# Attention into a phase mixer on one core: the first batch's head ordered by hand, its bias added by matmul, its first loads on hardware queues

## The chip, the cores and the metric

The kernel runs on one core of a Trainium2 chip. The metric is the device time of one execution in microseconds (us). Every execution also has a record of the TensorE clock that was granted to it, as a share of full speed. Executions are sorted into fast and slow, and only fast ones are compared here. In the profile PE is TensorE, PEld its weight loads, DVE VectorE, ACT ScalarE, POOL GpSimd, and SP the queue engine.

## The reference

Four batches of attention with eight heads are followed by a mixing layer. What matters of it, cut:

```python
B, H, S, D = 4, 8, 768, 64                     # q, k, v: [B, H, S, D] float32
dist = np.where(is_global & ~is_local, n_local, abs(i - j))
bias = -slopes[:, None, None] * dist           # slopes = 2 ** -(h + 1)
a = softmax(q @ k.T / 8 + bias, where keep = (j < 8) | (0 <= i - j < 96))
x = (a @ v)                                    # -> [B, S, 512]
theta = x @ w_theta
y = w_tok_r @ (x * cos(theta)) + w_tok_i @ (x * sin(theta))
u = x + y
out = u + relu(u @ w_ch)
```

The mask is a band, so for each tile of 128 keys the kernel computes only the scores of that tile's own 128 queries and of the next tile's; there are six such tiles, and all but the last have both parts.

## The kernel before

The work is done for pairs of heads ("pair" from here on; four pairs to a batch). Per pair, `prep` copies q and k into the order that PE transposes, and DVE or ACT copies them out of PSUM as qT and kT; kG is a copy of kT with the eight global keys put in. `scores` does the matmuls for a third of the tiles, one exp on ACT, and one multiply on DVE with `etab`, which holds exp(bias). `values` multiplies with v, normalises and writes x. `xtrans` transposes x for `theta`, whose sines and cosines are the last ACT work before the mixing matmuls can run. I call everything up to the sixth sine and cosine of batch 0 the head. Cuts are marked.

```python
    alloc_loads(0)                      # all loads of q, k, v: POOL's software queue, float32 -> bf16
    load_qk(0, 0, 2); load_qk(0, 2, 2); load_v(0, 0, 4)
    load_qk(0, 4, 2); load_qk(0, 6, 2); load_v(0, 4, 4)
    # ... ident and dist from a scan, a transpose and comparisons, on DVE

    def bias_table(p):
        for h in (2 * p, 2 * p + 1):
            nc.scalar.activation(etab[:, h, 0:3], dist, AF.Exp, scale=-slopes[h])
        # ... two of the five blocks are copied on DVE

    def scores(b, p, c):
        # ... matmuls of qT with kT and kG into pb (PSUM), start=True, stop=True
        ins = nc.scalar.activation(e_c, pb[:, :, 0:n], AF.Exp, scale=scale).ins
        # ... behind the last exp of a batch: a small Sin, which loads the sine table early
        nc.vector.tensor_mul(e_c, e_c, tab[...])          # one of two forms

    # the head: order set by hand on PE alone, the other engines left to the scheduler
    with tc.manual_schedule(engines={mybir.EngineType.PE}):
        warm(8)                                            # matmuls on zeros
        prep(0, 0, 4)
        distances()
        bias_table(0)
        for p in range(1, NP + 1):
            if p < NP:
                prep(0, p, 2 if p == 1 else 0)
                bias_table(p)
            if p == 2:
                vglob(0, 0, 4)                             # vG: copy of v with the global keys
            if p == 3:
                vglob(0, 4, 4)
            for c in range(NT // 2):
                scores(0, p - 1, c)
                if p == 1:
                    warm(1)
            if p > 1:
                values(0, p - 2, 0)
                values(0, p - 2, 1)
            if p > 2:
                xtrans(0, p - 3, nc.scalar.copy)
        # ... the last values, xtrans, and the first transposed token weights
    # ... then theta(0), and mixing of batch b woven with the attention of batch b + 1
```

The softmax here doesn't subtract the row's maximum and nothing guards it: scores larger than these inputs give would overflow.

Of the kernel before, what the change touches and what calls it, by code (L numbers as in the profile page):

```python
# [9 lines left out]
FP = mybir.dt.float32  # L10
BF = mybir.dt.bfloat16
# [5 lines left out]
def kernel(  # L17
# [61 lines left out]
                            in_=v[b, h0:h0 + n].rearrange("h (t p) d -> p (h t) d", p=T))  # L79


    alloc_loads(0)
    load_qk(0, 0, 2)
    load_qk(0, 2, 2)
    load_v(0, 0, 4)
    load_qk(0, 4, 2)
    load_qk(0, 6, 2)
    load_v(0, 4, 4)
    zero = const.tile([T, 512], BF)
    nc.vector.memset(zero, 0.0)  # L90

    ones = const.tile([T, 2 * T], FP)
    nc.vector.memset(ones, 1.0)
    ramp = const.tile([T, 2 * T], FP)
    nc.vector.tensor_tensor_scan(ramp, ones, ones, -1.0, op0=ALU.mult, op1=ALU.add)
    kmod = const.tile([T, GS], FP)
    nc.vector.transpose(kmod, ramp[:, 0:GS])
    pidx = const.tile([T, 1], FP)
    for p in range(NP):
        nc.vector.tensor_scalar(pidx[GS * p:GS * (p + 1), :], kmod[GS * p:GS * (p + 1), 0:1],  # L100
                                float(GS * p), None, op0=ALU.add)
    ident = const.tile([T, T], BF)
    nc.vector.tensor_scalar(ident, ramp[:, 0:T], pidx, None, op0=ALU.is_equal)






    assert NG <= T - NL and NG <= GS  # L110
    dist = const.tile([T, 3, T], FP)
    far = const.tile([T, 2 * T], FP)
    near = const.tile([T, 2 * T], FP)

    def distances():
        nc.vector.tensor_scalar(near, ramp, pidx, None, op0=ALU.subtract)
        nc.vector.tensor_scalar(far, near, 0.0, None, op0=ALU.is_lt)
        nc.vector.scalar_tensor_tensor(far, in0=near, scalar=float(NL), in1=far,
                                       op0=ALU.is_ge, op1=ALU.add)
        nc.vector.scalar_tensor_tensor(dist[:, 2], in0=far[:, 0:T], scalar=1e6, in1=near[:, 0:T],  # L120
                                       op0=ALU.mult, op1=ALU.max)
        nc.vector.scalar_tensor_tensor(dist[:, 1], in0=far[:, T:2 * T], scalar=1e6,
                                       in1=near[:, T:2 * T], op0=ALU.mult, op1=ALU.max)
        nc.vector.tensor_copy(out=dist[:, 0], in_=dist[:, 2])
        nc.vector.tensor_scalar(dist[0:NG, 0], dist[0:NG, 2], float(NL), None, op0=ALU.min)
        nc.vector.memset(dist[0:NG, 1], float(NL))


    etab = const.tile([T, H, 5, T], BF)

    def bias_table(p):
        for h in (2 * p, 2 * p + 1):
            nc.scalar.activation(etab[:, h, 0:3], dist, AF.Exp, scale=-slopes[h])
        hs = slice(2 * p, 2 * p + 2)
        nc.vector.tensor_copy(out=etab[:, hs, 3:5], in_=etab[:, hs, 1:3])

    halfpi = const.tile([T, 1], FP)
    junk = const.tile([T, 1], FP)
# [34 lines left out]

    anchor = {}

    def behind(eng):

        return tc.issue_after(anchor[eng]) if eng in anchor else nullcontext()

    def prep(b, p, w=0):  # L180
        qk = loads[b][0]
        if (b, 0) not in qkT:
            x_sb[b] = moe.tile([T, NP, NT, T], BF, name="x_sb", bufs=2)
            xT_sb[b] = moe.tile([T, NC, S], BF, name="xT", bufs=1)

        qkn = att.tile([T, NT, 2, 2, D], BF, name="qkn", bufs=3)
        with behind("dve"):
            for i_ in range(2):
                (nc.scalar.copy if b == 0 and i_ and p < 2 else nc.vector.tensor_copy)(  # L189
                    out=qkn[:, :, i_].rearrange("p t h d -> p h t d"), in_=qk[:, i_, 2 * p:2 * p + 2])  # L190
        qT = att.tile([T, S], BF, name="qT", bufs=6)
        kT = att.tile([T, S], BF, name="kT", bufs=6)
        kG = att.tile([T, NT - 2, T], BF, name="kG", bufs=6)
        for i_, dst in ((0, qT), (1, kT)):
            ps = ps_small([T, NT, T], BF)
            with behind("pe"):
                for t_ in range(NT):
                    nc.tensor.transpose(ps[:, t_, :], qkn[:, t_, i_].rearrange("p h d -> p (h d)"), ident)  # L198

            dst = dst.rearrange("p (n t) -> p n t", t=NT)  # L200
            src = ps.rearrange("p t n -> p n t")
            if i_ == 0:
                nc.vector.tensor_copy(out=dst, in_=src)  # L203
            else:
                nc.scalar.copy(out=dst, in_=src)  # L205
            if w:
                warm(w)

        nc.vector.tensor_copy(out=kG, in_=kT[:, T:(NT - 1) * T].rearrange("p (t n) -> p t n", t=NT - 2))
        nc.vector.tensor_copy(out=kG[:, :, 0:NG], in_=kT[:, None, 0:NG].to_broadcast([T, NT - 2, NG]))  # L210
        qkT[(b, p)] = (qT, kT, kG)

    ebuf = {}

    def scores(b, p, c):
        qT, kT, kG = qkT[(b, p)]
        if c == 0:
            ebuf[(b, p)] = att.tile([T, 2, NT, 2, T], BF, name="e", bufs=4)
        e_t = ebuf[(b, p)]
        pb = ps_big()  # L220
        for j in range(2):
            jt = 2 * c + j
            own = slice(jt * T, (jt + 1) * T)
            nxt = slice((jt + 1) * T, (jt + 2) * T)
            for part in range(2 if jt + 1 < NT else 1):
                for hh in range(2):
                    R = slice(D * hh, D * (hh + 1))
                    lhsT = kG[R, jt - 1, :] if part and jt else kT[R, own]
                    o = (2 * j + part) * T
                    nc.tensor.matmul(pb[:, hh, o:o + T], lhsT=lhsT, rhs=qT[R, (own, nxt)[part]],  # L230
                                     start=True, stop=True)
        n = min(4, 2 * NT - 1 - 4 * c) * T
        e_c = e_t[:, :, 2 * c:2 * c + 2].rearrange("p a j s n -> p a (j s n)")[:, :, 0:n]
        ins = nc.scalar.activation(e_c, pb[:, :, 0:n], AF.Exp, scale=scale).ins  # L234
        if c == NT // 2 - 1 and p == NP - 1:

            with tc.issue_after(ins):
                nc.scalar.activation(junk, halfpi, AF.Sin)
        tab = etab[:, 2 * p:2 * p + 2]
        if c == 0 or n < 4 * T:  # L240
            s0 = 0 if c == 0 else 2
            nc.vector.tensor_mul(e_c, e_c, tab[:, :, s0:s0 + n // T].rearrange("p a s n -> p a (s n)"))  # L242
        else:
            e4 = e_t[:, :, 2 * c:2 * c + 2].rearrange("p a j s n -> p a j (s n)")
            nc.vector.tensor_mul(
                e4, e4, tab[:, :, 2:4].rearrange("p a s n -> p a (s n)")[:, :, None, :].to_broadcast(
                    [T, 2, 2, 2 * T]))

    vGs, pos = {}, {}

# [52 lines left out]

    def theta(b, c, j):
        if c == 0 and j == 0:
            zri[b] = moe.tile([T, 2, NT, DM], BF, name="zri", bufs=1)
        xT, xb = xT_sb[b], x_sb[b]
        if j == 0:
            pss["th"] = ps_big()
# [5 lines left out]
        if j == 1:  # L315
            cs = moe.tile([T, 2, 2, DM], BF, name="cs")
            nc.scalar.activation(cs[:, 0], pb, AF.Sin, bias=halfpi)  # L317
            nc.scalar.activation(cs[:, 1], pb, AF.Sin)
            for i_ in range(2):
                for j_ in range(2):  # L320
                    nc.vector.tensor_mul(  # L321
                        zri[b][:, i_, 2 * c + j_, :].rearrange("p (g d) -> p g d", g=NP),
                        xb[:, :, 2 * c + j_, :],
                        cs[:, i_, j_].rearrange("p (g d) -> p g d", g=NP))
# [81 lines left out]

    load_w()
    load_all(1)
    with tc.manual_schedule(engines={mybir.EngineType.PE}):
        warm(8)  # L410
        prep(0, 0, 4)
        distances()
        bias_table(0)
        for p in range(1, NP + 1):
            if p < NP:
                prep(0, p, 2 if p == 1 else 0)
                bias_table(p)
            if p == 2:
                vglob(0, 0, 4)
            if p == 3:  # L420
                vglob(0, 4, 4)
            for c in range(NT // 2):
                scores(0, p - 1, c)
                if p == 1:
                    warm(1)
            if p > 1:
                values(0, p - 2, 0)
                values(0, p - 2, 1)
            if p > 2:
                xtrans(0, p - 3, nc.scalar.copy)  # L430
        values(0, NP - 1, 0)
        values(0, NP - 1, 1)
        xtrans(0, NP - 2, nc.scalar.copy)
        xtrans(0, NP - 1, nc.scalar.copy)
        trans_w(0, nc.scalar.copy)
    rest = []
    for b in range(B):
        nxt = b + 1 if b + 1 < B else None
# [3 lines left out]
        th = [lambda c=c, j=j: theta(b, c, j) for c in range(NT // 2) for j in range(2)]  # L442
        pre = [lambda p=p: prep(nxt, p) for p in range(NP)] if nxt else []
        if b == 0:
            order = th
        elif nxt:
            order = rest[:-1] + pre[:2] + th[:2] + pre[2:] + th[2:3] + rest[-1:] + th[3:]
        else:
# [20 lines left out]
            rest.insert(1, lambda b=b: utrans(b, NT - 1))  # L469
    for f in rest:  # L470
        f()


# [33 lines left out]
```

## Time and profile before

| kernel before | us |
|---|---|
| time, median of the first 3 runs | 190.88 (190.42 to 191.08) |
| span of the profiled run | 189.6 |
| first exp of batch 0 starts | 14.41 |
| last exp of batch 0 ends | 29.33 |
| first of the six sines and cosines starts | 35.49 |
| the sixth ends | 41.56 |
| first exp of batch 1 starts | 54.22 |

These are the milestones. The first lines of the page of the kernel before give busy time by engine; the rows of digits give the busy share of 40 equal slices in tenths, and PEclk is the granted clock, also in tenths:

```profile
PE 167.9 (89%) x1500; PEld 89.1 (47%) x1523; DVE 137.9 (73%) x309; ACT 102.9 (54%) x122; POOL 27.1 (14%) x31
...
PE   7855787899999999999939999999999999999981
...
PEclk9999669999999999999987999999999999999999
```

From the ninth slice (38 us) on, PE is full except for one stretch near 95 us, so the span after the head is PE's. In the head PE has digits of 5 to 8. An earlier end of the head therefore moves the whole rest forward. The same head in windows, for the kernel before (columns: the window, its length, busy us of PE, PEld, DVE, ACT, POOL with counts, then the clock, the DMA share and GB/s):

```profile
10.00:20.00 10.00, 5.88 (x95) 4.01 (x95) 7.62 (x21) 8.25 (x13) 5.89 (x8) 1.00 1.63 189
20.00:30.00 10.00, 8.20 (x131) 6.73 (x128) 8.83 (x24) 8.85 (x12) 3.99 (x3) 0.66 1.16 209
```

Over these windows no engine is full, DVE and ACT both run near 9 of 10 us in the second one, and the clock falls to 0.66 there. Windows of half the length show more: from 15 to 25 us DVE is busy all the time (5.00 of 5 us twice) and ACT nearly so (5.00 and 4.80). The chain of waits of the kernel before in the head (start, duration, what; each piece released the next):

```profile
4.20 8.16 DMA vn<-in_v_dram
...
12.38 0.43 DVE vG L259
12.81 0.20 DVE kG L209
...
14.41 2.64 ACT e L234 x3
...
18.15 0.94 ACT e L234
...
19.13 0.34 PE pb L230 x6
19.47 0.92 PE ps L278 x22
20.39 1.29 PE ps L198 x12
...
21.71 0.80 ACT kT L205
22.51 0.94 ACT e L234
```

The first exp waits, through kG, for v: the scheduler put the vG copy ahead of the kG copy on DVE, and v lands at 12.36. And from 18 us on the chain goes round a loop of ACT and PE once a pair: exp, scores (L230), values (L278), the twelve transposes of the next pair (L198), the kT copy, exp. One turn is 22.51 - 18.15 = 4.4 us. PE's weight loads and matmuls are not the limit in themselves: PE had idle time in both windows.

### The profile page before, as it was taken

The page shows a single profiled execution, that of the slowest core. Times are in us where ns is not written, and L with a number is a line of the kernel's source. Part 1 is how long each engine was busy: PE and PEld are TensorE (multiplying, and loading weights), DVE is VectorE, ACT ScalarE, POOL GpSimd, SP SyncE. Part 2 cuts the span into 40 slices and gives each one's busy share as a digit, 9 for nine tenths or more (in the row PEclk, how much of TensorE's full clock was granted, in tenths as well). Part 3 has the DMA queues.
Part 4 walks back from the last instruction along what each step waited for, and adds up shares of the span by engine and source line. Part 5 has one row for each costly group of instructions (what it writes and reads, how often), then busy time and mean ns, then how long its engine had stood idle before and what let it go on. Part 6 is the DMA issues. An engine that isn't in the chain of part 4 may idle for free.

```text
span 189.6 us, 3693 instructions
## 1 busy us (share of the span) xinstructions
PE 167.9 (89%) x1500; PEld 89.1 (47%) x1523; DVE 137.9 (73%) x309; ACT 102.9 (54%) x122; POOL 27.1 (14%) x31
## 2 busy tenths in 40 slices
PE   7855787899999999999939999999999999999981
PEld 2424665445656555654414454644454544434430
DVE  5839987386999997998853786998877864734422
ACT  2469988871397684598724360499663604800010
POOL 7974361300040004020000000000000000000000
PEclk9999669999999999999987999999999999999999
DMA  4999999999999983999991337301165374113432
GB/s 63 153 188 181 210 209 207 204 189 142 130 83 182 225 116 75 148 142 146 223 116 58 74 91 185 109 3 55 28 66 141 88 145 148 59 32 107 118 106 111
DMA packets 58081, 23.97 MB, mean 126 GB/s; under 512 B 44240, under 2 KB 54992, under 8 KB 58064
## 3 DMA queue, kind: packets, MB, share of 16 engines
q0 software_dynamic: 35760, 12.85, 70.6%
q1 hardware_dynamic: 22304, 10.88, 25.0%
q8 instruction: 12, 0.20, 0.5%
q14 instruction: 5, 0.04, 0.1%
HBM read 25.69 MB, written 6.29 MB: 169 GB/s over the span
## 4 chain that ended last, share of the span: by engine, by line
PE 55%; ACT 14%; DVE 13%; DMA 12%; issue 2%; POOL 2%; ACTq 0%; POOLq 0%
PE ps L332 22%; PE ps L357 10%; DMA uT<-u 8%; PE pb L313 7%; ACT e L234 6%; PE pb L230 5%; DMA vn<-in_v_dram 4%; PE pb L278 4%; DVE qT L203 4%; ACT cs L317 3%; PE ps L198 3%; DVE qkn L189 2%; PE ps L278 2%; DVE zri L321 2%; POOL qk L72 2%
## 5 line engine op out<-in xcount | busy, mean ns | idle before, releaser
L234 ACT ACTIVATE e<-pb 128x1024 bf16<-128x1024 f32 (+1 forms) x48 | 44.1, 958 | 25.8 <-PE pb L230 25.7
L332 PE MATMUL ps<-zri,w_tokT_111 128*128 128x512 bf16 x141 | 53.6, 381 | 0.9 <-issue 0.3
L332 PE MATMUL ps<-zri,w_tokT_110 128*128 128x512 bf16 x130 | 49.5, 382 | 1.3 <-DVE zri L321 0.8
L337 DVE TENSOR_TENSOR u<-x_sb,ps 128x512 bf16<-128x512 bf16 x24 | 16.5, 687 | 16.6 <-PE ps L332 16.0
L357 PE MATMUL ps<-w_ch_bf,uT 128*128 128x512 bf16 x94 | 25.3, 391 | 3.7 <-DMA uT<-u 3.5
L360 DVE SCALAR_TENSOR_TENSOR o_sb<-ps,u 128x512 f32<-128x512 f32 x24 | 16.5, 687 | 11.4 <-PE ps L357 11.4
L313 PE MATMUL pb<-w_theta_bf,xT 128*128 128x512 bf16 x93 | 23.6, 379 | 0.7 <-ACT xT L299 0.4
L321 DVE TENSOR_TENSOR zri<-x_sb,cs 128x512 bf16<-128x512 bf16 x48 | 18.3, 421 | 7.2 <-ACT cs L317 6.1
L242 DVE TENSOR_TENSOR e<-e,etab 128x1024 bf16<-128x1024 bf16 (+1 forms) x32 | 19.7, 617 | 3.5 <-ACT e L234 3.5
L230 PE MATMUL pb<-qT,kT 64*128 64x128 bf16 x224 | 17.9, 231 | 4.7 <-ACT e L234 4.6
L332 PEld LDWEIGHTS <-w_tokT_110 128*128 128x128 bf16 x144 | 14.1, 98 | 15.2 <-issue 1.1
L332 PEld LDWEIGHTS <-w_tokT_111 128*128 128x128 bf16 x144 | 14.1, 98 | 13.2 <-issue 0.5
L205 ACT COPY kT<-ps 128x768 bf16<-128x768 bf16 x16 | 12.9, 805 | 13.4 <-PE ps L198 13.4
L230 PEld LDWEIGHTS <-kT 64*128 64x128 bf16 x224 | 10.0, 99 | 18.3 <-issue 16.7
L351 ACT COPY uT<-ps 128x512 bf16<-128x512 bf16 x7 | 4.1, 587 | 26.1 <-PE ps L350 26.1
L317 ACT ACTIVATE cs<-pb,halfpi 128x1024 bf16<-128x1024 f32 x12 | 13.4, 1120 | 8.9 <-issue 6.8
L278 PEld LDWEIGHTS <-e 128*128 128x128 bf16 x352 | 14.7, 100 | 6.8 <-issue 1.0
L198 PE MATMUL ps<-ident,qkn 128*128 128x128 bf16 x192 | 16.1, 232 | 1.1 <-DVE qkn L189 0.9
L198 PEld LDWEIGHTS <-qkn 128*128 128x128 bf16 x192 | 12.8, 103 | 8.4 <-DVE qkn L189 6.1
L230 PE MATMUL pb<-qT,kG 64*128 64x128 bf16 x128 | 13.6, 228 | 2.0 <-DVE kG L210 2.0
L203 DVE COPY qT<-ps 128x768 bf16<-128x768 bf16 x16 | 15.2, 947 | 0.0
L357 PEld LDWEIGHTS <-uT 128*128 128x128 bf16 x96 | 8.4, 99 | 13.5 <-DMA uT<-u 4.7
(63 smaller groups left out, 204.3 us busy)
## 6 DMA issues: line engine op xcount, KB each, us to landing
out_dram<-o_sb SPq DMA_DIRECT2D x24, 256.0 KB, 2.3
qk<-in_q_dram POOLq DMA_DIRECT2D x3, 768.0 KB, 8.1
qk<-in_k_dram POOLq DMA_DIRECT2D x3, 768.0 KB, 13.6
vn<-in_v_dram POOLq DMA_DIRECT2D x3, 768.0 KB, 22.7
w_nat<-in_moe_w_tok_r_dram POOLq DMA_DIRECT2D x3, 384.0 KB, 13.6
w_nat<-in_moe_w_tok_i_dram POOLq DMA_DIRECT2D x3, 384.0 KB, 14.8
qk<-in_q_dram POOLq DMA_DIRECT2D x4, 192.0 KB, 6.4
qk<-in_k_dram POOLq DMA_DIRECT2D x4, 192.0 KB, 6.7
```

Of the source, the lines that this page charges most:

```text
L198: nc.tensor.transpose(ps[:, t_, :], qkn[:, t_, i_].rearrange("p h d -> p (h d)"), ident)
L203: nc.vector.tensor_copy(out=dst, in_=src)
L230: nc.tensor.matmul(pb[:, hh, o:o + T], lhsT=lhsT, rhs=qT[R, (own, nxt)[part]], start=True, stop=True)
L234: ins = nc.scalar.activation(e_c, pb[:, :, 0:n], AF.Exp, scale=scale).ins
L242: nc.vector.tensor_mul(e_c, e_c, tab[:, :, s0:s0 + n // T].rearrange("p a s n -> p a (s n)"))
L278: nc.tensor.matmul(o, lhsT=l_, rhs=r_, start=(i_ == 0), stop=(i_ == len(mms) - 1))
L313: nc.tensor.matmul(pb[:, j, :], lhsT=xT[:, dc, st * T:(st + 1) * T], rhs=w_theta_bf[:, dc, :], start=(dc == 0), stop=(dc == NC - 1))
L317: nc.scalar.activation(cs[:, 0], pb, AF.Sin, bias=halfpi)
L321: nc.vector.tensor_mul(zri[b][:, i_, 2 * c + j_, :].rearrange("p (g d) -> p g d", g=NP), xb[:, :, 2 * c + j_, :], cs[:, i_, j_].rearrange( ...
L332: anchor["pe"] = nc.tensor.matmul(ps, lhsT=w_tokT[wi][:, st, tt * T:(tt + 1) * T], rhs=zri[b][:, wi, st, :], start=(st == 0 and wi == 0), ...
L337: anchor["dve"] = nc.vector.tensor_add(u_sb[b, tt].rearrange("p (g d) -> p g d", g=NP), x_sb[b][:, :, tt, :], ps.rearrange("p (g d) -> p g ...
L357: nc.tensor.matmul(ps_c, lhsT=uT[:, dc, :], rhs=w_ch_bf[:, dc, :], start=(dc == 0), stop=(dc == NC - 1))
```

## The change

The intent is a shorter head: order every engine by hand there, get the first q and k sooner, take work off DVE and ACT. In five parts:

1. **Loads.** q and k of pair 0 come as float32 through hardware queues (issued by SP and ACT), and are cast on chip. The other loads stay on POOL's software queue.
2. **Bias on PE.** In batch 0 the bias is put into PSUM by a matmul (a diagonal of -slope/scale times `dist`), and the score matmuls add to it. The twelve multiplies with `etab` go. So do 17 of the 23 warm-up matmuls.
3. **Tables out of the head.** `etab` is needed from batch 1 on only, so its eight exps come behind the sixth sine, 640 columns wide for 384 before.
4. **Order.** Casts of pair p+2 and its transposes are issued one pair earlier, kG never stands behind vG.
5. **Set-up.** An iota on POOL replaces a scan on DVE for `ident` and `dist`.

The core of the diff, with cuts:

```diff
-    load_qk(0, 0, 2)
+    qk32 = moe.tile([T, 2, 2, NT, D], FP, name="qk32", tag="zri", bufs=1)
+    for i_, eng in ((1, nc.sync), (0, nc.scalar)):
+        eng.dma_start(out=qk32[:, i_]..., in_=(q, k)[i_][0, 0:2]...)
+    nc.gpsimd.iota(near, pattern=[[1, 2 * T]], base=0, channel_multiplier=-1, ...)
 ...
+    def score_bias(p, c):
+        pb = pbs[0, p, c] = ps_big()
+        for hh in range(2):
+            nc.tensor.matmul(pb[:, hh, 0:n * T], lhsT=diag[:, 2 * p + hh],
+                             rhs=dist[:, s0:s0 + n]..., start=True, stop=False)
 ...
-                                     start=True, stop=True)
+                                     start=bool(b), stop=bool(b) or (...))
 ...
+        if b == 0:
+            return                       # no multiply with etab in batch 0
 ...
-    with tc.manual_schedule(engines={mybir.EngineType.PE}):
-        warm(8)
-        prep(0, 0, 4)
-        ...
+    warm(6)                              # all five engines by hand
+    distances(); diagonals(0)
+    # pair 0: casts, transposes and copies split in halves over DVE and ACT
+    kglob(0, 0)
+    score_bias(0, 0); score_bias(0, 1)
+    score_mms(0, 0, 0); score_mms(0, 0, 1)
+    score_exp(0, 0, 0)
+    # casts, diagonals and transposes of pair 1
+    for p in range(NP):
+        nxt = p + 1 < NP
+        score_exp(0, p, 1)
+        if nxt:
+            out0(p + 1, 1, act)          # kT on ACT
+            out0(p + 1, 0, dve)          # qT on DVE
+            kglob(0, p + 1)
+        if p:
+            values(0, p - 1, 0); values(0, p - 1, 1)
+        score_bias(p, 2); score_mms(0, p, 2); score_exp(0, p, 2)
+        if p + 2 < NP:
+            # casts on DVE, diagonals(p + 2)
+        # vglob(0, 0, 4) at p == 0, vglob(0, 4, 4) at p == 1
+        if nxt:
+            # scores 0 and 1 of pair p + 1, exp 0
+            if p + 2 < NP:
+                turn0(p + 2, 1); turn0(p + 2, 0)
+        if p:
+            xtrans(0, p - 1, act if p == NP - 1 else dve)
+    # ... values, trans_w, xtrans, theta(0)
+    for p in range(NP):
+        bias_table(p)
```

## The prediction

> **What bounds the kernel now.** The span is 189.6 us. From 37 us on it is TensorE's: the windows show PE busy 95 to 99% from 40 to 80 us and from 100 to 160 us. Before that nobody is full (10 to 20 us: PE 5.9, DVE 7.6, ACT 8.3). The chain of waits in this head runs POOL issues (to 4.2 us), the v load (lands 12.4), DVE copies, first exp at 14.4, then exps in groups of three at 14.4, 18.0, 22.4, 26.7 (a period of 4.1 us), last exp ending 29.3, six sines from 35.5 to 41.6, full mixing from about 42.5. The first exp is late because kG stands behind vG, which waits for v. The DMA share is 99% nearly everywhere from 5 to 55 us; batch 1's q and k land at 39.0 and 42.9 and are first cast at 46.9.
>
> **What the change does.**
> - DVE loses 12 etab multiplies in batch 0 (0.54 to 0.68 us, 7.6 us) and the scan chain (about 1.6 us); it gains 8 small diagonals and xT copies.
> - ACT loses two 0.83 us casts, and the tables (3.9 us) move behind the sines, wider (640 for 384 columns: estimate 8 x 0.65 us plus one 1.28 us table load).
> - PE gains 24 bias matmuls of 512 or 384 columns (0.216 us step warm, 0.43 as in the first warm-ups: 4.8 to 9 us) and loses 17 warm-ups.
> - k0 and q0 come through hardware queues: estimate landed by 4 to 4.6 us, against 4.7 and 6.7.
> - kG no longer stands behind v.
>
> Replaying the new order by hand with these durations: with a quick iota the first exp starts at about 7.5 us, the sines end at 35 to 39 us, against 41.6: 3 to 6 us gained, all critical, as the later PE-bound phase merely starts earlier.
>
> **The catch.** The changed program has a library reload on POOL ahead of the iota; the old has none. The Trainium skill, "GPSIMD Engine Reference", section Instruction dispatch, gives about 6 us for the first call to a freshly loaded kernel; this trace cannot check it. If it holds, ident, dist and every software-queue load come some 6 to 7 us later: the first exp at 13 to 14 us, v at 17 to 18, the last exp at 30 to 32, the sines end at 41 to 45, batch 1's k lands near 48. The gain is then gone, up to 3 us worse. I hold that more likely than not (0.6).
>
> **Second risk.** Warm-ups vanish. The granted clock falls to 0.66 from 20 to 30 us even so; the skill's "TensorE: Matmul & The Clock Gate", Part 1, says idleness halves the clock. Cold, the bias matmuls put PE on the head's critical path.
>
> **Time.** Quick iota: about 186. Slow: about 191.5. Together 189.5, range 184.5 to 196. Faster by over 2%: 0.31; within 2%: 0.45; slower: 0.24.
>
> **What would show it.** POOL's timeline: does the first software load issue before 3 us or after 8? The first exp's start; the end of the sixth sine; PE idle before batch 1's transposes (late loads); the granted clock from 10 to 35 us; uT copies behind the eight table exps.
>
> **What would make it wrong.** A hidden reload; a clock that stays low; a changed collision of uT transposes with loads (the chain holds 8.6 us of it at 90 us).

## The result, and the profile after

The changed kernel took 186.06 us (median of 4 runs, 185.80 to 186.38), the kernel before 190.98 beside it (190.42 to 192.26). The ratio is 0.9731, with a 95% interval of 0.9688 to 0.9775: faster. Here and below a ratio is the mean time of one kernel's fast runs over that of the other's fast runs of the same rounds, so it is not quite the ratio of the medians that I quote.

| milestone in the profiled run, us | before | after | gain |
|---|---|---|---|
| first exp starts | 14.41 | 9.31 | 5.10 |
| last exp of batch 0 ends | 29.33 | 25.14 | 4.19 |
| first sine starts | 35.49 | 29.93 | 5.56 |
| sixth ends | 41.56 | 36.01 | 5.55 |
| first exp of batch 1 | 54.22 | 48.77 | 5.45 |
| span | 189.6 | 184.0 | 5.6 |

The gain is complete at the sixth sine and is carried to the end unchanged. It does not come from a faster pace of the pairs: from the first exp to the end of the last the four pairs took 14.92 us before and 15.83 after. The changed kernel starts 5.1 us earlier, gives 0.9 of it back, and wins 1.4 between the last exp and the first sine. The same lines of the page, for the kernel after:

```profile
PE 166.5 (90%) x1505; PEld 86.9 (47%) x1530; DVE 134.4 (73%) x299; ACT 102.3 (56%) x120; POOL 25.6 (14%) x30
...
PE   5889879999999999998769999999999999999981
...
PEclk9999999999999999999978999999999999999998
```

Busy totals hardly moved, so this is not less work but less waiting: PE's digits reach 8 in the second slice and 9 from the seventh. The windows of the kernel after, same columns:

```profile
10.00:20.00 10.00, 8.85 (x139) 5.66 (x138) 8.51 (x26) 8.77 (x11) 4.43 (x7) 1.00 1.56 193
20.00:30.00 10.00, 8.39 (x117) 5.07 (x119) 6.63 (x18) 6.60 (x9) 4.05 (x3) 1.00 1.16 209
```

PE does 8.85 us in place of 5.88 between 10 and 20 us, and DVE and ACT have become free for a third of the next window, with the multiplies and tables gone and the last exp over by 25.14 us. The clock stays at 1.00. The chain of waits in the head of the kernel after:

```profile
0.74 4.19 DMA qk<-in_k_dram
4.95 0.52 ACT qkn L187
...
5.52 1.46 PE ps L193 x12
6.98 1.71 PE pb L246 x4
...
9.31 1.94 ACT e L273 x2
11.25 0.70 ACT kT L200
...
14.75 0.70 ACT kT L200
...
16.11 0.56 DVE x_sb L333
```

The wait for v is gone; the first exp now hangs on k's load, its cast, the transposes and four bias matmuls (L246). The first two kT copies on this chain lie 3.5 us apart, in place of the old loop's 4.4, but that is not the average: see the 15.83 us above. From 15.5 to 22.5 us the chain then stays on DVE, without a gap. The later stages have the old shape: the one stall of PE, at a DMA transpose of u, lasts 8.63 us after and 8.61 before.

### The profile page after: what moved, and what is told of

Same layout as the page of the kernel before. It is cut to its first block, busy times and chain, and to the rows that moved or that the text cites. A ratio compares the mean times of both kernels' runs of the same rounds, so it can differ in the third digit from the quotient of the medians.

```text
span 184.0 us, 3698 instructions
## 1 busy us (share of the span) xinstructions
PE 166.5 (90%) x1505; PEld 86.9 (47%) x1530; DVE 134.4 (73%) x299; ACT 102.3 (56%) x120; POOL 25.6 (14%) x30
## 4 chain that ended last, share of the span: by engine, by line
PE 55%; DVE 14%; ACT 14%; DMA 9%; issue 6%; ACTq 0%
PE ps L377 23%; PE ps L402 10%; DMA uT<-u 6%; ACT e L273 5%; PE pb L358 5%; PE pb L266 5%; PE pb L323 4%; ACT cs L362 4%; PE ps L225 4%; DVE x_sb L333 3%; DMA qk<-in_k_dram 2%; ACT cs L363 2%; DVE zri L366 2%; PE ps L157 1%; DVE qT L230 1%
## 5 line engine op out<-in xcount | busy, mean ns | idle before, releaser
L377 PE MATMUL ps<-zri,w_tokT 128*128 128x512 bf16 x271 | 70.0, 383 | 1.6 <-issue 0.6
L377 PEld LDWEIGHTS <-w_tokT 128*128 128x128 bf16 x288 | 25.5, 98 | 28.3 <-issue 1.7
L266 PEld LDWEIGHTS <-kT 64*128 64x128 bf16 x224 | 9.1, 95 | 17.4 <-issue 14.9
L396 ACT COPY uT<-ps 128x512 bf16<-128x512 bf16 x7 | 4.1, 586 | 22.5 <-PE ps L395 22.4
L283 DVE TENSOR_TENSOR e<-e,etab 128x1024 bf16<-128x1024 bf16 (+1 forms) x24 | 14.8, 617 | 1.9 <-ACT e L273 1.7
L232 ACT COPY kT<-ps 128x768 bf16<-128x768 bf16 x12 | 9.7, 808 | 10.5 <-PE ps L225 10.3
L78 POOL DMA_DIRECT2D vn<-in_v_dram x5 | 9.6, 1915 | 29.7 <-DVE rec L331 17.1
L358 PEld LDWEIGHTS <-xT 128*128 128x128 bf16 x96 | 8.8, 98 | 10.1 <-issue 1.3
L323 PE MATMUL pb<-vn,e 128*128 128x65 bf16 x168 | 12.2, 195 | 0.6 <-ACT e L273 0.4
L363 ACT ACTIVATE cs<-pb 128x1024 bf16<-128x1024 f32 x12 | 12.3, 1026 | 0.0
L333 DVE TENSOR_TENSOR x_sb<-pb,rec 128x768 bf16<-128x768 f32 x12 | 11.5, 955 | 0.3
## 6 DMA issues: line engine op xcount, KB each, us to landing
w_nat<-in_moe_w_tok_i_dram POOLq DMA_DIRECT2D x3, 384.0 KB, 15.5
```

The costliest lines, as they stand in the source:

```text
L266: nc.tensor.matmul(pb[:, hh, o:o + T], lhsT=lhsT, rhs=qT[R, (own, nxt)[part]], start=bool(b), stop=bool(b) or (jt == NT - 1 or (j == 1 and ...
L323: nc.tensor.matmul(o, lhsT=l_, rhs=r_, start=(i_ == 0), stop=(i_ == len(mms) - 1))
L333: nc.vector.tensor_mul(xv, po4[:, :, :, 0:D], rec.to_broadcast([T, n, NT, D]))
L358: nc.tensor.matmul(pb[:, j, :], lhsT=xT[:, dc, st * T:(st + 1) * T], rhs=w_theta_bf[:, dc, :], start=(dc == 0), stop=(dc == NC - 1))
L363: ins = nc.scalar.activation(cs[:, 1], pb, AF.Sin).ins
L377: anchor["pe"] = nc.tensor.matmul(ps, lhsT=w_tokT[wi][:, st, tt * T:(tt + 1) * T], rhs=zri[b][:, wi, st, :], start=(st == 0 and wi == 0), ...
```

## The experiments

Twelve kernels ran, all with correct results. The milestones are of the profiled run. "Mean" is of the timed fast runs. Means are compared only with the ratio's own partners: the kernel before took 190.47 as a mean beside e1 to e4, 192.05 beside e5 to e8, 190.46 beside e9 to e11, 191.26 beside e12.

| run | what | first exp | last exp ends | sixth sine ends | span | mean | ratio to before (95%) |
|---|---|---|---|---|---|---|---|
| before | | 14.41 | 29.33 | 41.56 | 189.6 | | 1 |
| after | | 9.31 | 25.14 | 36.01 | 184.0 | 186.08 | 0.9731 (0.9688 to 0.9775) |
| e1_swload | after, software loads | 10.93 | 27.45 | 38.33 | 186.4 | 187.93 | 0.9866 (0.9797 to 0.9935) |
| e2_dvebias | after, multiplies and tables back | 9.36 | 29.76 | 42.24 | 189.3 | 192.34 | 1.0097 (0.9968 to 1.0226) |
| e3_bfence | before, kG ahead of vG | 12.27 | 29.53 | 43.01 | 191.2 | 193.20 | 1.0142 (1.0081 to 1.0204) |
| e4_warm10 | after, ten warm-ups | 9.32 | 25.41 | 36.30 | 184.7 | 185.38 | 0.9713 (0.9628 to 0.9799) |
| e5_bwarm | before, more fillers | 14.57 | 29.42 | 41.67 | 188.5 | 190.57 | 0.9923 (0.9874 to 0.9972) |
| e6_bfencewarm | e3 and e5 together | 11.63 | 29.20 | 41.45 | 187.8 | 189.18 | 0.9851 (0.9798 to 0.9903) |
| e7_biota | before, an unused iota | 16.80 | 29.55 | 41.84 | 189.9 | 193.00 | 1.0050 (0.9979 to 1.0121) |
| e8_tabhead | after, tables back | 9.37 | 26.33 | 39.29 | 185.7 | 188.38 | 0.9809 (0.9757 to 0.9861) |
| e9_kgact | after, first kG on ACT | 8.36 | 24.52 | 35.4 | 183.3 | 185.16 | 0.9732 (0.9652 to 0.9812) |
| e10_kgact10 | e9 and e4 together | 8.41 | 24.35 | 35.2 | 184.0 | 184.73 | 0.9709 (0.9623 to 0.9795) |
| e11_combo | e10 and more off DVE | 8.43 | 24.17 | 34.9 | 183.5 | 185.54 | 0.9751 (0.9678 to 0.9825) |
| e12_bpebias | before, bias on PE | 14.70 | 29.68 | 41.14 | 188.2 | 189.68 | 0.9906 (0.9867 to 0.9945) |

The theories at the start were these. The **start** theory: the old head was late because kG stood behind v; an earlier first exp is the gain. The **loads** theory: it is the hardware-queue loads. The **DVE** theory: it is the removed multiplies and tables. The **clock** theory: it is the half clock between 20 and 30 us. And the open branch of the prediction: what the iota costs POOL.

### e7_biota: the old kernel with an iota that nothing uses

```diff
+    idle = const.tile([T, 2 * T], FP)
+    nc.gpsimd.iota(idle, pattern=[[1, 2 * T]], base=0, channel_multiplier=-1,
+                   allow_small_or_imprecise_dtypes=True)
     alloc_loads(0)
```

> The old kernel with one unused iota, and so one library reload, on POOL ahead of all loads. My prediction's slow branch says that the first software load is issued 6 us or more later and the total is 195 us or more. The changed kernel's trace (iota 0.33 us, 0.4 us of wait ahead of it) says 0.3 to 0.6 us later and a total within 0.7 us of the old kernel.

POOL's timeline has it (start, duration, engine, line, operation), first of the kernel before, then of e7, then of the kernel after:

```profile
1.25 0.81 POOL L72 DMA_DIRECT2D qk<-in_q_dram  x1 [0.81 <-POOLq L488]
```

```profile
0.84 0.34 POOL L83 IOTA idle<- 128x256 f32 x1 [0.39 <-POOLq L491]
1.35 0.84 POOL L72 DMA_DIRECT2D qk<-in_q_dram  x1 [0.18 <-issue]
```

```profile
0.84 0.33 POOL L92 IOTA near<- 128x256 f32 x1 [0.39 <-POOLq L578]
1.36 0.84 POOL L72 DMA_DIRECT2D qk<-in_q_dram  x1 [0.19 <-issue]
```

The iota starts at 0.84 us and the first software load is issued at 1.35, only 0.10 us later than without it. The time, 1.0050 with an interval that holds 1, shows no cost of several us. The first exp came later here, at 16.80, but the last exp did not (29.55), which is a first hint of a result below. It is no more than a hint, because the scheduler also reordered the rest: all eight table exps ran from 6.10 us on, ahead of the first exp, where the kernel before had spread them over the pairs. So the branch that I had held more likely fell: in these runs the iota and its reload together put the first load off by about 0.1 us. What can be seen of a reload: the traces of both runs hold two MODIFY_POOL_CONFIG instructions of POOL's queue, of 11 ns each, at 0.74 and 0.78 us (the timeline leaves them out, a query by the iota's line lists them), and the kernel before has none. The iota starts 0.05 us after the second. Whether code was loaded ahead of the span, or was there already, these records do not show.

### e1_swload: the changed kernel with pair 0 on the software queue again

```diff
-    qk32 = moe.tile(...)
-    for i_, eng in ((1, nc.sync), (0, nc.scalar)):
-        eng.dma_start(out=qk32[:, i_]..., ...)
     alloc_loads(0)
+    load_qk(0, 0, 2, (1, 0))
     load_qk(0, 2, 2)
-        src = qk32[:, i_] if p == 0 else loads[0][0][:, i_, 2 * p:2 * p + 2]
+        src = loads[0][0][:, i_, 2 * p:2 * p + 2]
```

> The changed kernel, only its first pair back on the software queue (bf16, k first, then q; everything else as changed). If the hardware loads carry the gain, the first exp starts about 2.5 us or more later than the changed kernel's 9.3 us and the total is 188.5 us or more. If the order and the bias carry it, k and q land within about 1.5 us of the hardware loads (the old kernel's first two took 3.5 and 4.6 us from issue), the first exp is about 1 us later and the total is 186.5 to 187.5 us.

The casts of e1 on ACT show when k and q were there:

```profile
4.95 0.51 ACT L184 COPY qkn<-qk 128x384 bf16<-128x384 bf16 x1 [2.93 <-DMA qk<-in_k_dram]
7.25 0.51 ACT L184 COPY qkn<-qk 128x384 bf16<-128x384 bf16 x1 [1.79 <-DMA qk<-in_q_dram]
```

k came no later than in the changed kernel (cast at 4.95 in both). q came at 7.25; in the changed kernel the cast of q starts by 5.4. The two loads land 2.3 us apart on the software queue and nearly together on the two hardware queues. The first exp is 1.6 us later, the last exp, the sines and the span 2.3 to 2.4 us. That lies between what the order and the loads theories expected: about 2.4 of the 5.6 us hang on the loads, and the rest does not. Pair 0 is not the whole of it. With pair 0 back on the software queue all later loads are issued behind it, and the chain of waits of e1 runs through k of pair 2 (issued at 6.45, in the changed kernel at 5.06):

```profile
6.45 8.77 DMA qk<-in_k_dram
```

DVE sat idle for 1.15 us before the cast of it at 15.24, where the changed kernel had this cast at 12.39 without a wait. So moving two loads to other queues also brought the loads of the other pairs forward.

### e2_dvebias: the changed kernel with multiplies on DVE and tables on ACT in the head

```diff
-    score_bias(0, 0)
-    score_bias(0, 1)
+    bias_table(0)
 ...
+        score_mul(0, p, 0)
+        score_mul(0, p, 1)          # the multiplies with etab, three per pair
 ...
-    for p in range(NP):
-        bias_table(p)               # behind the sines
```

> The changed kernel, with batch 0's bias back as a multiply on DVE and the tables back on ACT in the head; loads and hand order kept, no bias matmuls. If the bias on PE matters for the pace of the four pairs, DVE (7.6 us more) and ACT (5 us more) lengthen the head by 3 to 5 us: 189 to 191 us, and with fewer matmuls the granted clock dips below 1.0 between 10 and 30 us as it did before. If only the early start matters, the first exp stays near 9 us and the total within 1 us of 186.

The first exp is as early as in the changed kernel, 9.36, and the last exp ends at 29.76, later than in the kernel before. The sixth sine ends 6.2 us later than in the changed kernel. So in this form an early start is worth nothing at the end of the head. The chain of waits of e2, one pair's turn and the transposes before and after it:

```profile
14.29 1.48 PE ps L193 x12
...
15.78 0.96 DVE qT L200
...
17.15 0.59 DVE e L287
17.74 0.60 DVE e L290
...
20.06 1.46 PE ps L193 x12
```

DVE carries qT, kG (cut), two multiplies and x (cut) in one line, and the transposes take 1.46 to 1.48 us, as they do at half clock. The windows of e2 give a clock of 0.85 from 20 to 30 us and 0.81 from 30 to 40, where the changed kernel has 1.00. Even that is too kind: the trace's first record of a full clock in e2 is at 23.55 us (8.93 in the changed kernel), the views print the unrecorded time before it as 1.00, and the transposes at 14.29 and 20.06 say that PE was still at half clock. e8 below, which has the bias matmuls, keeps 1.00 in both. That suggests that they also keep PE warm, with 17 warm-ups fewer. It also means that e2 does not measure multiplies and tables alone: three groups of transposes on its chain took 1.41 to 1.48 us where one at full clock took 0.84 (e9), so by an estimate from these figures about 1.8 us of its delay are the clock's. The timed mean has only two fast runs (191.03 and 193.65) and carries less weight than the milestones.

### e8_tabhead: only the tables back in the head

```diff
         score_exp(0, p, 2)
+        bias_table(p)
 ...
-    for p in range(NP):
-        bias_table(p)
```

> The changed kernel with only the exp tables moved back into the head, two (0.65 us each) behind the last exp group of each pair on ACT; bias stays on PE. If ACT has no room there, the pairs' period rises from 4.05 to 4.7 us, the last exp ends 2 to 2.5 us later and the total is 187.5 to 188.5 us, although 6.4 us of tables behind the sines are gone. If ACT's gaps take them in, the total is within 0.5 us of 186.

The last exp moved by 1.2 us, less than expected; the total of 188.41 as median was as expected, but partly for another reason. The chain of waits of e8 behind the last exp:

```profile
26.34 1.28 ACT L277
...
27.85 1.28 ACT L131
...
31.91 1.28 ACT L362
```

These are three loads of ACT's function table. My edit put the last pair's tables behind the small sine that loads the sine table early, so exp and sine tables were loaded once more each. Of the 3.3 us by which the sixth sine came later, about 2.6 (2 x 1.28) are my edit's own fault, so e8 overstates what tables cost at that milestone. And its span lost only 1.7 us: it had no clock dip near 100 us (see e5 below), and no tables behind the sines. What stands is the last exp: the tables cost the head 1.2 us there. In e2 tables, multiplies and the half clock together cost 4.6; an estimate for the multiplies and the clock against bias on PE, inside the new order, is the difference, 3.4 us, if they add. With the 1.8 us put down to the clock above, some 1.6 would be left for the multiplies; no run separates the two.

### e3_bfence: the old kernel with vG held behind the first kG

```diff
+        kg_ins[b, p] = nc.vector.tensor_copy(
+            out=kG[:, :, 0:NG], in_=kT[:, None, 0:NG].to_broadcast([T, NT - 2, NG])).ins
 ...
-        with behind("dve"):
+        with tc.issue_after(kg_ins[0, 0]) if b == 0 and h0 == 0 else behind("dve"):
```

> The old kernel, with one fence: vG of the first four heads comes behind kG of the first pair on DVE, so that the first scores no longer wait for v. If the DVE order is what made the first exp late, it starts near 12.3 us in place of 14.4, and if the pace then holds, the total falls by about 2 us to 189. If the pairs are paced by DVE, ACT or the clock, the start moves and the last exp does not: under 0.5 us gained.

The first exp came 2.1 us earlier, the last exp 0.2 us later, and the kernel was slower (1.0142). The windows of e3, as above:

```profile
20.00:30.00 10.00, 8.31 (x121) 7.19 (x119) 9.78 (x25) 7.14 (x9) 4.75 (x4) 0.50 1.16 209
```

The start theory falls as far as an early first exp alone goes: DVE is full (9.78) from 20 us on although the exps began earlier, and PE is at half clock for the whole window. That left a doubt that the clock had eaten the gain, which e5 and e6 were made for. A third cause shows in the trace, and I had not asked for it: between 11 and 17 us DVE sat idle for 2.9 us in front of casts of pairs 2 and 3 that waited for their q and k (2.18, 0.50 and 0.19 us), while the first multiply, whose exp had long ended, stood behind these casts in its queue and began at 16.91.

### e5_bwarm and e6_bfencewarm: the old kernel with fillers, without and with the fence

```diff
                 scores(0, p - 1, c)
-                if p == 1:
-                    warm(1)
+                if p < 4:
+                    warm(1 if p == 1 else 2)
```

e6 is this edit and e3's.

> The old kernel with filler matmuls behind the scores of pairs 1 and 2 too (two per group, as it already has one per group for pair 0). If the half clock from 20 to 27 us is on the path of the old head, the granted clock stays near 1.0 there, the last exp ends 1 us or more before 29.3 us and the total falls by about 1 us. If the pairs are paced by DVE and ACT alone, the clock rises and nothing else changes (under 0.4 us).

> The old kernel with the vG fence of the earlier run and the fillers as well. The fence alone started the first exp 2.1 us earlier and lost it all, with the granted clock at 0.50 from 20 to 30 us. If the clock ate it, this run ends its last exp at 27 to 28 us and the total is about 2 us below the old kernel. If DVE and ACT ate it, the last exp stays at 29 us or later and the total is not below the old kernel's.

The fillers did raise the clock to 1.00 from 20 to 30 us in both runs. The last exp ended at 29.42 and 29.20, against 29.33: nothing was gained in the head. So taking away the late start, the low clock or both was not enough in the old kernel. The chain of waits of e6 says what came next (cut):

```profile
7.72 8.48 DMA qk<-in_k_dram
...
16.22 0.36 DVE qkn L190
16.58 0.60 DVE e L244
```

In e6 it is first the load of pair 3's k, which lands at 16.19 and whose cast stands ahead of the first multiply on DVE (DVE idled 2.98 us in front of pair 2's casts as well), and then DVE with the twelve multiplies, 9.67 us busy of 10 from 20 to 30. In the old kernel's runs with the multiplies the first of them began at 16.05 (before), 16.53 (e5), 16.49 (e6), 16.91 (e3) and 17.86 us (e7), whenever the first exp came, and the last exp ended within 0.4 us in all five. The chain of the kernel before runs through the ACT and PE loop of 4.4 us instead, but DVE is full there too. So several limits lie close together: the load of pair 3 with the casts ahead of the multiplies, DVE's work behind it, and the loop. An early start with the multiplies ahead of those casts was not run, so it stays open what it would gain.

Yet both runs were faster by the clock on the wall, e5 by 0.8%, e6 by 1.5%, with heads that had not moved. Comparing later milestones settles where, for the profiled runs. From the start of batch 1's last cosine pair (third activation with the half-pi bias) to the start of batch 2's first lie 36.58 us in the kernel before, 35.44 in e5 and 34.98 in e6. The windows there, first of the kernel before, then of e5:

```profile
90.00:100.00 10.00, 6.60 (x66) 3.10 (x66) 6.45 (x12) 4.58 (x6) 0.00 (x0) 0.92 1.08 163
100.00:110.00 10.00, 9.90 (x99) 4.87 (x100) 6.07 (x10) 4.45 (x5) 0.00 (x0) 0.91 0.31 85
```

```profile
90.00:100.00 10.00, 6.25 (x67) 3.01 (x67) 6.53 (x12) 4.67 (x6) 0.00 (x0) 1.00 1.15 166
100.00:110.00 10.00, 9.89 (x112) 5.38 (x114) 6.69 (x11) 4.91 (x5) 0.00 (x0) 1.00 0.36 95
```

PE stalls on the DMA transpose of u in both (6.60 and 6.25 us busy of 10), and behind the stall it runs at half clock for a while in one and not in the other. Over the profiles of before, after and all twelve experiments, the four without a dip in these two windows (e2, e5, e6, e8) take 35.0 to 35.4 us for this stretch, the ten with one take 36.1 to 36.9. The means are 35.2 and 36.6, so a dip goes with about 1.4 us. e5 and e6 changed no work there, and the shorter stretch is 1.1 of the 1.1 us that e5's span gained and 1.6 of e6's 1.8. Why they had no dip just there these runs do not show. The Trainium skill, "TensorE: Matmul & The Clock Gate", Part 1, describes a clock that halves after an idle window of about 3.4 us, with the windows running freely and so falling differently from run to run. This trace agrees: the missing clock in the two windows, 0.08 and 0.09 of 10 us, is 1.7 us, or 3.4 us at half clock, and the clock record of the packed trace has it as one stretch of 3.41 us at 0.50.

The same shows in the timed runs of the kernel before: over its 27 fast runs beside the experiments, the time falls by 1.0 us for every 0.01 of mean clock (a straight fit, correlation -0.83). At the changed kernel's clock, 0.989, the fit gives 189.9 us for the old kernel, against 186.1 measured for the new. So some 3.8 of the 4.9 us are there at equal clock, and up to 1.1 may go with fewer dips. This is a fit over runs, not an experiment. In the two profiled runs of before and after themselves the stretch is equal (36.58 and 36.74), so that the 5.6 us between their spans are the head's.

### e12_bpebias: the old kernel with the bias on PE, and nothing else

```diff
+        if b == 0:
+            for hh in range(2):
+                nc.tensor.matmul(pb[:, hh, 0:m * T], lhsT=diag[:, 2 * p + hh],
+                                 rhs=dist[:, s0:s0 + m]..., start=True, stop=False)
 ...
-                                     start=True, stop=True)
+                                     start=bool(b), stop=bool(b) or (...))
 ...
+        if b == 0:
+            return                  # no multiplies in batch 0; tables stay in the head
```

> The old kernel with one part of the change alone: batch 0's bias added by PE (dist in bf16, eight diagonals, 24 bias matmuls) and its 12 multiplies on DVE gone; loads, scan, tables in the head on ACT, scheduler and the late first exp all as before. In five runs with the multiplies on DVE the last exp ended between 29.2 and 29.8 us, whether the first exp started at 9.4 or at 16.8 us. If DVE's work set that end, it now ends at 27.5 us or earlier, and since the late start then shows, not as early as the changed kernel's 25.1; total 1.5 to 3 us below the old kernel. If ACT's tables or the loads set it, the last exp stays at 29 us or later and the total within 0.5 us. If the bias were the whole gain, last exp near 25 us and total near 186.

DVE's busy time from 20 to 30 us fell from 8.83 to 6.05, and the last exp stayed where it was: 29.68. My DVE theory, that the multiplies alone paced the old head, falls. The chain of waits of e12:

```profile
19.27 0.92 ACT e L251
...
20.24 0.48 PE pb L235 x2
...
21.77 0.68 PE ps L208 x12
...
22.48 0.80 ACT kT L215
```

It is the loop of ACT and PE again, now with the bias matmuls (L235) in it; PE is at full clock and the twelve transposes take 0.68 us for 1.29, which pays for the bias and no more. A turn still takes 4.0 us. Ahead of these lines, from 14.70 to 20.19 us, the chain is on ACT without a gap, with three table exps in it (0.41, 0.41 and 0.42 us): what the expectation called ACT's tables is a part of this floor too. The order of the changed kernel, which has the transposes done a pair ahead, takes them out of the loop, and its tables are gone from it as well; e12 does not tell the two apart. The sines end 0.4 us earlier and the total is 0.9% lower.

### e4_warm10, e9_kgact, e10_kgact10 and e11_combo: can the changed kernel's start be shortened?

In the changed kernel the twelve transposes and the four bias matmuls of pair 0 ran at half clock (1.46 and 1.71 us). e4 has ten warm-ups for six. e9 has the first kG copied by ACT instead of DVE. e10 is both. e11 also makes all diagonals early and moves xT copies from DVE to ACT.

```diff
-    warm(6)
+    warm(10)                        # e4, e10, e11
-    kglob(0, 0)
+    kglob(0, 0, act)                # e9, e10, e11
```

```diff
+    for p in range(1, NP):
+        diagonals(p)                # e11, ahead of the q transposes of pair 0
 ...
+        if p > 1:
+            xts[p - 2]()            # e11: the xT copy on ACT, one step later
```

> The changed kernel with ten warm-up matmuls in place of six, so that PE is busy from 1.2 us to the first transposes at 5.5 us. If PE's slow clock is on the path to the first exp (its 12 transposes took 1.46 us against 0.84 later, its first four bias matmuls 1.7 us against 0.86), the first exp comes about 1 us earlier and the total is 185 us. If loads and casts set it alone: no change.

> The changed kernel with kG of the first pair copied by ACT and not by DVE, whose copy took 0.77 us (0.28 elsewhere) and ended with the long POOL issue of v. Alone it should give little, under 0.3 us: PE, still at half clock, is at its bias matmuls until 8.7 us. If the slow kG alone holds the first exp, it comes 0.4 us earlier.

> kG of the first pair on ACT, and ten warm-ups in place of six. With ten warm-ups alone PE had its first scores at 8.0 us and then waited for kG until 9.05 us. If these two are the two holders of the first exp, together they bring it from 9.3 to about 8.7 us, and the total to about 0.6 us below the changed kernel's. If the pace of the pairs is set by DVE's work, the start moves and the last exp does not: no gain.

> As the run before, and DVE relieved in the four pairs: all diagonals made while DVE waits for the first transposes (0.6 us), xT copies of the first two pairs on ACT (1.1 us). If DVE's order of copies sets the pace there, the last exp ends 1 to 1.5 us before 25.1 us and the total is 184.5 to 185 us. If ACT or the loads set it, no change against the run before, or 0.5 us worse as ACT gets more work.

In e4 PE was warm (transposes 0.92 us, bias 1.03), and the first exp did not move: 9.32. DVE's kG copy was the second floor at the same height. The timelines of DVE and of POOL in the kernel after at that time, then that of ACT in e9:

```profile
8.00 0.77 DVE L206 COPY kG<-kT 128x512 bf16<-128x512 bf16 x1
```

```profile
7.19 1.47 POOL L78 DMA_DIRECT2D vn<-in_v_dram  x1
```

```profile
7.16 0.62 ACT L206 COPY kG<-kT 128x512 bf16<-128x512 bf16 x1 [0.21 <-DVE kT L200]
```

That copy mostly takes 0.28 us elsewhere. Here it takes 0.77 and ends at 8.77, just after POOL has done issuing the load of v (7.19 + 1.47 = 8.66). In e4 it took 0.95. The Trainium skill, "SBUF — State Buffer", section Who interferes with whom, says that a DVE copy in its two-port mode and a GpSimd instruction take a shared pair of ports for themselves alone, and that the later one waits. The trace agrees for this copy, with DVE as the one that waits. It does not hold for every overlap: in the kernel before the same copy took 0.28 us at 12.73, although POOL was issuing a load from 12.65 to 13.37.

e9 was a miss of mine: I had expected less than 0.3 us and got 0.95 at the first exp. In that run PE happened to be warm by 5.5 us with six warm-ups, where the changed kernel's PE was not until about 8.9. Against e4, with PE as warm, the place of kG is worth 0.96 us. e10 and e11 keep this, and e11's sines end 1.1 us earlier than in the changed kernel. In the time of the whole kernel nothing of it is resolved: 0.9732, 0.9709 and 0.9751 against 0.9731 for the changed kernel, with intervals of about 0.8% to each side. e11's expected 184.5 to 185 was missed with 185.56 as median. None of these versions clearly beats the changed kernel.

## Why the prediction was right or wrong

**The result lay in the range, on the branch that I held less likely.** The prediction had two branches, "quick iota: about 186" and "slow: about 191.5", and gave the slow one 0.6. The figure of 189.5 was their mixture. The measured 186.06 is the quick branch. The range of 184.5 to 196 held both, so that the result lies in it says nothing for my choice between them; that choice was wrong.

**The step that failed** is this: "about 6 us for the first call to a freshly loaded kernel ... If it holds, ident, dist and every software-queue load come some 6 to 7 us later ... I hold that more likely than not (0.6)." The runs showed in its place an iota of 0.33 us at 0.84 us, and the first software load at 1.36 for 1.25: 0.11 us late. e7, with the iota alone, had 0.10. The two MODIFY_POOL_CONFIG instructions are there, at 0.74 and 0.78 us, and no 6 us follow them. I had carried a stated figure to a situation in which it did not show.

**The quick branch held, point by point.** "The sines end at 35 to 39 us": 36.01. "3 to 6 us gained, all critical, as the later PE-bound phase merely starts earlier": 5.55 at the sixth sine and 5.6 in the span.

**The first exp was mis-sized**: "at about 7.5 us" became 9.31. The terms that were too small are the transposes (1.46 us against 0.92 when warm, in e4), the bias matmuls (1.71 against 1.03) and the kG copy beside POOL's load issue (0.77 against 0.28). They sum to 1.7 us, though e4 showed that the PE terms and the copy ran side by side rather than in a row. The loads were near: "landed by 4 to 4.6 us", and k landed at 4.93.

**The reason for the late first exp was right, and I gave it too much weight.** kG did stand behind vG. But e3 and e6 took that away in the old kernel and gained nothing at the last exp, with DVE then waiting for the loads of pairs 2 and 3; e2 has the early start and loses all of it, at half clock.

**"DVE loses ... 7.6 us" was right for its item** (4 x (0.686 + 0.679 + 0.548) = 7.7), but DVE's busy total fell by 3.5 us only, for it got diagonals, casts and xT copies. e12 shows that this loss is worth nothing at the last exp with the old order, loads and tables.

**"Cold, the bias matmuls put PE on the head's critical path"** came true for pair 0 only: the clock was 1.00 from 10 us on, and e2 suggests that the bias matmuls themselves kept it there.

**The collisions did not come.** The uT copy stood behind the eight table exps, at 42.35 us directly after them, but the first exp of batch 1 was still 5.45 us earlier than before. The stall at the DMA transpose kept its 8.6 us. Batch 1's first cast moved forward, from 46.92 to 41.77.

**What the gain is made of** is shown only in part. Inside the changed kernel the hardware loads are worth 2.3 us at the sixth sine (e1), bias on PE and tables out of the head together 6.2 (e2, of which part is its half clock). Their sum exceeds the whole 5.55. In the old kernel the earlier kG and the bias on PE are worth nothing or 0.4 (e3, e6, e12). The parts do not add. My reading is that the old head had several floors close together: DVE with the multiplies, the loads of pairs 2 and 3 with the casts that wait for them ahead of the multiplies, and the loop of ACT, with its tables, and PE. That reading comes from the chains of before, e3, e6, e12 and after. No run has the new order alone or the tables alone taken out of the old kernel, so which part of the order matters is not shown. Open as well is what ten warm-ups are worth by themselves, as the number of cold microseconds at the start differed from run to run.

## What to carry to other kernels

When a chain of waits names one late event, move that event alone and look at the end of the stage before believing in it: here the first exp moved from 11.6 to 16.8 us in the old kernel, and the last exp stayed within 0.4 us, since other limits of the stage lay at nearly the same height. Then read the new run's chain from its beginning: in e3 and e6 the wait that took the place of the first one was a load of a later pair, and the end of the chain alone does not show it. Here removing work from one engine (e12) or moving one start (e3, e6) paid little, and the change that did all of it at once paid 5.6 us. And before reading a total of 1% as the effect of an edit, compare the granted clock in stages that the edit does not touch: one dip there was worth more than 1 us.

## What the Trainium skill lacked or had wrong

- "GPSIMD Engine Reference", section 2.1 Instruction dispatch, gives about 6 us for the first call to freshly loaded code, with no visible instruction. Neither the kernel after nor e7 shows it: the iota starts at 0.84 us and the next load issue is 0.10 to 0.11 us later than without it. The page names the gap by which it was measured, from MODIFY_POOL_CONFIG to the first instruction behind it; in these two runs that gap is 0.05 us. It does not say when the cost is not paid.
- "ScalarE: Activation LUTs", section What ACT_TABLE_LOAD costs, gives about 1.28 us for the load and about 1.38 us more for a drain, 2.66 for each switch. The load agrees (1.28 us). The drain is not seen in these runs: the load at 36.03 us in the kernel after is followed by the first table exp at 37.33, 0.02 us after its end.
- "SBUF — State Buffer", section Who interferes with whom, says that either side can be the one that waits. It does not say at what part of a software load's issue POOL holds DVE up. In these runs a kG copy of 0.28 us took 0.77 to 0.95 and ended about 0.1 us after an issue of some 1.5 us (after, e4, e6), and one of 0.28 us in the kernel before ran at 12.73 inside an issue without delay. No page that I consulted gives the length of such an issue (about 0.7 us for a 192 KB load of q or k and for a 384 KB load of w_nat, 1.47 us for a 384 KB load of v).
- "TensorE: Matmul & The Clock Gate", Part 1, advises not to fit the ramp, as under 1% of a typical span. The figure holds here, but it does not warn of what it means for comparing two kernels: a single half-clock stretch behind a stall at 90 to 110 us goes with about 1.4 us of 190, which is 0.7% and as large as several of the effects measured here.
